# Reordering the opening loads of a one-core kernel: two x tiles side by side, w_in blocks whole behind them, both tiles transposed first, the gate row third on ScalarE's queue

## The chip, the cores and the metric

The kernel runs on one core of a Trainium2 chip. The metric is device time in microseconds (us); several executions of each kernel are compared with executions of the kernel before on the same chip, in the same rounds. Executions are called fast or slow; a slow one is over 1.5% above the fastest of its kernel, and only fast ones are compared.

A few names: PE is TensorE (matmuls), PEld its weight load, ACT ScalarE, DVE VectorE, POOL GpSimd, SP the queue that issues most loads. A name with q (SPq) is an engine's instruction queue. L192 is a source line.

## The reference, cut to what matters

The result is a gated mix of a linear-attention branch and a gMLP branch over x (2048 x 512, bf16). This case is about the first product of the gMLP branch and the gate:

```python
z = _gelu(jnp.einsum('bsd,df->bsf', x, w_in))     # w_in: 512 x 1376, halves z1 | z2
z2 = _layernorm(z[..., Fh:], axis=-1)             # Fh = 688
g = _sigmoid((x * gate_w).sum(-1, keepdims=True))
return g * a + (1 - g) * b                        # a: attention, b: gMLP
```

The contraction runs over 512 = 4 blocks of 128 rows of w_in ("block 0" to "block 3"). x is cut into 16 tiles of 128 rows; each must be transposed before it can be the stationary operand. The gate's weights are a 689th column of w_in's z2 half.

## The kernel before: the parts that matter

Tiles 0 and 1 of x are loaded plainly and transposed on TensorE; tiles 2 and later come through transposing loads.

```python
nc.gpsimd.dma_start(out=gaterow[0:NDT, :], in_=gate_w...)             # gate row, GpSimd
nc.sync.dma_start(out=xs[:, 0, :], in_=x2[0:P, :])                    # x tile 0
nc.scalar.dma_start(out=w_z2[:, 0, 0:HF], in_=...)                    # block 0, first half
nc.sync.dma_start(out=xs[:, 1, :], in_=x2[P:2 * P, :])                # x tile 1
load_z2w(nc.scalar, 1)                                                # block 1
load_z2w(nc.sync, 2)                                                  # block 2
nc.scalar.dma_start(out=w_z2[:, 0, HF:FH], in_=...)                   # block 0, second half
load_z2w(nc.sync, 3)                                                  # block 3
...
x_dma_T(2, 2)                                                         # x tiles 2 and 3, transposing, SP
# ... w_z1, x tiles 4 to 15, brow, wqkT, eight small w_phi loads, wv, wspT, all on SP
```

The order of TensorE's work on the two tiles is written out by hand. `warm_up` runs matmuls on constants ("fillers") whose results are thrown away; `one(tt, dt, j)` is tile tt, block dt, half j; `z_part` is a part of a second half; `gate_T` transposes the gate row and VectorE copies it into column 689.

```python
warm_up(6)                       # six 128x512 fillers
warm_up(2, P)                    # two 128x128 fillers
x_T(0, 0, 1, ...); x_T(0, 1, NDT, ...)          # tile 0: four transposes
warm_up(3, P)
one(0, 0, 0)
x_T(1, 0, 2, ...); x_T(1, 2, NDT, ...)          # tile 1: four transposes
one(0, 1, 0); warm_up(1, P); one(1, 0, 0); one(1, 1, 0)
for tt in range(2): z_part(tt, 1, 0, HF, True)  # block 1, second half
gate_T()
for tt in range(2): z_part(tt, 0, 0, HF, False) # block 0, second half: the late load
# ... block 2, the gate column of blocks 0 and 1, block 3, outputs; then tile 2, tile 3, ...
```

The softmax here doesn't subtract the row's maximum and nothing guards it: scores larger than these inputs give would overflow.

## Time and profile before

| | before |
|---|---|
| time, median of 3 | 207.25 us (206.95 to 207.43) |
| span of the profiled execution | 205.4 us |
| PE busy | 201.2 us, 98% |
| PE's only wait inside the kernel | 0.47 us, for a load of w_in |

From the profile page: the span, the busy time of the first engines, and the chain of work that ended last, by engine.

```profile
span 205.4 us, 4012 instructions
PE 201.2 (98%) x1564; PEld 120.3 (59%) x1564; DVE 129.8 (63%) x282; ACT 75.4 (37%) x123; POOL 46.4 (23%) x77
...
PE 96%; DMA 2%; ACTq 0%; DVE 0%; issue 0%
```

PE's waits (what waited, for what, total us, times, longest): the first is the start of the program.

```profile
PE zp L223 <- PEq L627: 0.8, 1, 0.8
PE zp L231 <- DMA w_z<-in_B_w_in_dram: 0.5, 1, 0.5
```

So only the opening can be shortened. This is its timeline on PE (start in us, duration, engine and line, operation, count, and in brackets an idle time and what ended it). Matmuls overlap, so the distance between two starts tells the rate, not the duration. L223 are fillers, L285 transposes, L192 and L231 real matmuls, L295 the gate row.

```profile
3.57 0.63 PE L285 MATMUL pq<-ident,xs 128*128 128x128 bf16 x4
4.00 0.45 PE L223 MATMUL zp<-const-bfloat16-1.0 128*128 128x128 bf16 x3
4.28 0.31 PE L192 MATMUL zp<-w_z,xT 128*128 128x344 bf16 x1
4.43 0.27 PE L285 MATMUL tp<-ident,xs 128*128 128x128 bf16 x2
...
5.09 0.46 PE L192 MATMUL zp<-w_z,xT 128*128 128x344 bf16 x2
5.39 0.46 PE L231 MATMUL zp<-w_z,xT 128*128 128x344 bf16 x2
5.68 0.17 PE L295 MATMUL pq<-ident,gaterow 128*128 128x4 bf16 x1
6.32 0.45 PE L231 MATMUL zp<-w_z,xT 128*128 128x344 bf16 x2 [0.47 <-DMA w_z<-in_B_w_in_dram]
...
7.30 0.89 PE L192 MATMUL zp<-w_z,xT 128*128 128x344 bf16 x5
```

The second half of block 0 is issued at 1.74 us and lands at 6.28 us; PE is idle from 5.85 us. Transposes start 0.107 us apart at 3.57 us (four in 0.43 us); by 4.28 us, one 344-wide matmul takes 0.15 us to the next start. The clock rose at about 4.2 us. From 6.32 us on, a 344-wide matmul follows every 0.144 us. The last listed line holds block 3's four matmuls and the first of tile 2, so **tile 2 starts at 7.30 + 4 x 0.144 = 7.88 us**.

### The profile page before, as it was taken

How to read it: one execution, taken by the hardware profiler on the slowest of the kernel's cores; microseconds unless marked ns; L12 is line 12 of the kernel's file. 1: busy time of each engine (PE TensorE's matmuls, PEld its weight loads, DVE VectorE, ACT ScalarE, POOL GpSimd, SP SyncE). 2: the span in 40 equal slices, each digit the busy share in tenths (PEclk: the TensorE clock that was granted, in tenths of full speed). 3: DMA queues.
4: the chain of work that ended last, by engine and by line, in shares of the span. 5: the costliest groups of instructions: out<-in, count | busy, mean ns of one | idle time of the engine just before them, and what ended most of it. 6: DMA issues, size and time to landing. Idle time of an engine off the chain costs nothing.

```text
span 205.4 us, 4012 instructions
## 1 busy us (share of the span) xinstructions
PE 201.2 (98%) x1564; PEld 120.3 (59%) x1564; DVE 129.8 (63%) x282; ACT 75.4 (37%) x123; POOL 46.4 (23%) x77
## 2 busy tenths in 40 slices
PE   8999999999999999999999999999999999999994
PEld 4566666655665555656565666555555555665642
DVE  4377575747977687979797788555566645633330
ACT  3466577796222233332424042222251136002222
POOL 5020202020522425334242442222204220200000
PEclk9999999999999999999999999999999999999999
DMA  6998599999999017940433229763566568552942
GB/s 175 265 183 186 92 212 209 206 259 206 265 245 217 3 38 158 307 91 13 83 29 63 51 38 117 143 117 71 100 161 51 119 114 181 67 97 55 145 89 78
DMA packets 90100, 27.22 MB, mean 133 GB/s; under 512 B 84225, under 2 KB 90081, under 8 KB 90081
## 3 DMA queue, kind: packets, MB, share of 16 engines
q1 hardware_dynamic: 87312, 24.55, 64.1%
q10 hardware_dynamic: 2736, 2.42, 4.3%
q8 instruction: 12, 0.20, 0.4%
q14 instruction: 8, 0.06, 0.1%
q0 software_dynamic: 32, 0.00, 0.0%
HBM read 4.15 MB, written 2.10 MB: 30 GB/s over the span
## 4 chain that ended last, share of the span: by engine, by line
PE 96%; DMA 2%; ACTq 0%; DVE 0%; issue 0%
PE mm L459 36%; PE zp L192 18%; PE mm L360 14%; PE mm L520 8%; PE mm L514 7%; PE mm L400 7%; DMA w_z<-in_B_w_in_dram 2%; PE kvacc L416 2%; PE at L472 2%; PE mm L524 1%; PE zp L312 0%; PE at L483 0%; PE zp L231 0%; ACTq L118 0%; ACTq L121 0%; PE pq L312 0%
## 5 line engine op out<-in xcount | busy, mean ns | idle before, releaser
L459 PE MATMUL mm<-z2all,wspT 128*128 128x344 bf16 x512 | 79.9, 309 | 0.0
L459 PEld LDWEIGHTS <-wspT 128*128 128x128 bf16 x512 | 49.0, 98 | 25.3
L192 PE MATMUL zp<-w_z,xT 128*128 128x344 bf16 x252 | 37.9, 309 | 0.1
L364 ACT ACTIVATE eq<-mm 128x512 bf16<-128x512 f32 x32 | 17.4, 594 | 51.4 <-PE mm L360 25.7
L368 DVE TENSOR_REDUCE zs<-eq 128x64 f32<-128x1024 bf16 x16 | 19.5, 1220 | 20.1 <-ACT eq L364 20.1
L192 PEld LDWEIGHTS <-xT 128*128 128x128 bf16 x252 | 24.3, 98 | 12.0 <-DVE xT L291 0.3
L364 ACT ACTIVATE ek<-mm 128x512 bf16<-128x512 f32 x32 | 17.3, 601 | 27.1 <-PE mm L360 27.1
L377 POOL TENSOR_TENSOR eq<-eq,ratio 128x512 bf16<-128x512 bf16 x16 | 16.9, 1056 | 44.6 <-DVE ratio L376 36.7
L464 DVE SCALAR_TENSOR_TENSOR ucat<-mm,bT,z1all 128x344 bf16<-128x344 f32 x32 | 17.4, 544 | 14.9 <-PE mm L459 14.9
L535 ACT ACTIVATE ob<-mm,g_inv 128x512 bf16<-128x512 f32 (+1 forms) x16 | 10.9, 680 | 32.4 <-PE mm L524 26.6
L368 DVE TENSOR_REDUCE zs<-ek 128x64 f32<-128x1024 bf16 x16 | 19.3, 1209 | 2.8 <-ACT ek L364 2.8
L520 PE MATMUL mm<-wspT,uT 128*128 128x512 bf16 (+2 forms) x85 | 20.1, 367 | 0.0
L360 PEld LDWEIGHTS <-xT 128*128 128x128 bf16 x128 | 12.2, 98 | 12.0
L377 POOL TENSOR_TENSOR ek<-ek,ratio 128x512 bf16<-128x512 bf16 x16 | 16.9, 1056 | 2.2 <-DVE ratio L376 1.7
L514 PE MATMUL mm<-wspT,oT 128*128 128x512 bf16 (+2 forms) x68 | 16.6, 366 | 0.0
L360 PE MATMUL mm<-wq_p,xT 128*128 128x512 bf16 x64 | 16.4, 379 | 0.0
L400 PE MATMUL mm<-wv_sb,xT 128*128 128x512 bf16 x64 | 16.4, 379 | 0.0
L360 PE MATMUL mm<-wk_p,xT 128*128 128x512 bf16 x64 | 16.3, 379 | 0.0
L210 DVE BATCH_NORM_STATS2 bn<-z2all 128x6 f32<-128x344 bf16 x32 | 14.9, 503 | 0.0
L207 ACT ACTIVATE z2all<-zp 128x688 bf16<-128x688 f32 x16 | 11.8, 743 | 7.8 <-PE zp L192 7.7
L265 ACT ACTIVATE z1all<-zp 128x688 bf16<-128x688 f32 x16 | 11.9, 743 | 5.1 <-PE zp L192 4.7
L520 PEld LDWEIGHTS <-uT 128*128 128x128 bf16 x85 | 8.1, 98 | 9.4 <-issue 0.2
(78 smaller groups left out, 145.3 us busy)
## 6 DMA issues: line engine op xcount, KB each, us to landing
out_dram<-ob ACTq DMA_DIRECT2D x15, 128.0 KB, 2.2
wspT<-in_B_w_out_dram SPq DMA_DIRECT2D x2, 640.0 KB, 5.0
w_z<-in_B_w_in_dram SPq DMA_DIRECT2D x2, 344.0 KB, 4.8
wv_sb<-in_A_wqkv_dram SPq DMA_DIRECT2D x2, 256.0 KB, 3.6
wspT<-in_A_wo_dram SPq DMA_DIRECT2D x2, 256.0 KB, 4.0
w_z<-in_B_w_in_dram SPq DMA_DIRECT2D x2, 172.0 KB, 4.2
xs<-in_A_x_dram SPq DMA_DIRECT2D x2, 128.0 KB, 2.7
uT<-ucat SPq DMA_TRANSPOSE x16, 2.8
```

Source lines behind the costliest of these rows:

```text
L192: nc.tensor.matmul(zp[:, j, 0:n], lhsT=xT[:, dt, tt * P:(tt + 1) * P], rhs=wt[:, dt, j * HF:j * HF + n], start=(dt == first), stop=(dt == ...
L210: nc.vector.bn_stats(out=bn6[:, tt, j, :], in_=z2v[:, j, :])
L265: nc.scalar.activation(out=z1all[:, tt, :].rearrange("p (j n) -> p j n", j=2), in_=zp[:, :, 0:HF], func=AF.Gelu_apprx_tanh,)
L360: nc.tensor.matmul(ps[:, :], lhsT=xT[:, dt, tt * P:(tt + 1) * P], rhs=w[:, dt, :], start=(dt == 0), stop=(dt == NDT - 1))
L364: nc.scalar.activation(out=e[:, :, a, :], in_=ps[:, :].rearrange("p (h f) -> p h f", f=DH), func=AF.Exp, scale=1.0 - 2.0 * a)
L368: nc.vector.tensor_reduce(out=z[:].rearrange("p h a -> p (h a)"), in_=e[:].rearrange("p h a f -> p (h a) f"), axis=AX.X, op=ALU.add,)
L377: nc.gpsimd.tensor_tensor(out=e[:, :, 1, :], in0=e[:, :, 1, :], in1=ratio[:, :, None].to_broadcast([P, H, DH]), op=ALU.mult)
L400: nc.tensor.matmul(v_ps[:, :], lhsT=xT[:, dt, tt * P:(tt + 1) * P], rhs=wv_sb[:, dt, :], start=(dt == 0), stop=(dt == NDT - 1))
L459: nc.tensor.matmul(gp[:, 0:HF], lhsT=wspT[:, st, tt * P:(tt + 1) * P], rhs=z2all[:, st, j * HF:(j + 1) * HF], start=(st == 0), stop=(st == ...
L464: nc.vector.scalar_tensor_tensor(out=ucat[tt % NU][:, c0 + j * HF:c0 + (j + 1) * HF], in0=gp[:, 0:HF], scalar=bT[:, tt:tt + 1], in1=z1all[ ...
L514: nc.tensor.matmul(acc, lhsT=oTs[tt][:, g, :], rhs=wo_t[:, g, c0:c1], start=start and g == 0, stop=stop and g == NG - 1)
L520: nc.tensor.matmul(acc, lhsT=uTs[tt][:, i + ft, :], rhs=w_main[i][:, ft, c0:c1], start=start and ft == 0, stop=False)
```

## The change

Its intent: bring both x tiles in first, side by side on two queues, so that both can be transposed in one go; load block 0 whole, so that no late half stands in the way; move the gate row from GpSimd to ScalarE's queue, third; and drop fillers and the split matmuls that the late half needed. Long parts are cut.

```diff
-    nc.gpsimd.dma_start(out=gaterow[0:NDT, :], in_=gate_w...)
     nc.sync.dma_start(out=xs[:, 0, :], in_=x2[0:P, :])
-    nc.scalar.dma_start(out=w_z2[:, 0, 0:HF], in_=w_in_v[:, 0, FH:FH + HF])
-    nc.sync.dma_start(out=xs[:, 1, :], in_=x2[P:2 * P, :])
+    nc.scalar.dma_start(out=xs[:, 1, :], in_=x2[P:2 * P, :])
+    load_z2w(nc.sync, 0)
     load_z2w(nc.scalar, 1)
     load_z2w(nc.sync, 2)
-    nc.scalar.dma_start(out=w_z2[:, 0, HF:FH], in_=w_in_v[:, 0, FH + HF:F])
+    nc.scalar.dma_start(out=gaterow[0:NDT, :], in_=gate_w...)
     load_z2w(nc.sync, 3)
 ...
         warm_up(6)
-        warm_up(2, P)
+        warm_up(1, P)
         x_T(0, ...)
-        warm_up(3, P)
-        one(0, 0, 0)
         x_T(1, ...)
+        warm_up(2, P)
+        one(0, 0, 0)
+        z_part(0, 0, HF, True)
         one(0, 1, 0)
-        warm_up(1, P)
         one(1, 0, 0)
+        gate_T()
+        z_part(1, 0, HF, True)
         one(1, 1, 0)
         for tt in range(2):
-            z_part(tt, 1, 0, HF, True)
-        gate_T()
+            one(tt, 1, 1)
 ...     # then block 2 and block 3, in nearly the same order as before
```

## The prediction

> **What bounds it.** On the profile page PE is busy 98% of the 205.4 us span, and the chain of waits is 96% PE. The waits view of PE knows one wait inside the kernel: 0.47 us for a w_in DMA. Only the opening, until tile 2 begins, can shrink; the rest should shift with it.
>
> **The opening before** (timeline; DMA view, issue plus time to landing). Warm-ups run from 0.85 to 3.57 us. Landings, us: x tile 0 3.4; first half of w_in block 0 3.5; x tile 1 4.1; block 1 4.2; gate row 5.6; block 2 5.8; second half of block 0 6.3; block 3 6.5; x tiles 2 and 3 (transposing) 7.5. Real matmuls start at 4.28, broken up by tile 1's transposes and fillers; PE stops at 5.85 for the late half block, resumes at 6.32, and from there a matmul follows every 0.144 us. Tile 2 begins near 7.87. The two tiles need 16 such matmuls, 2.3 us.
>
> **What changes.** The same bytes before the transposing loads (966 KB at 260 to 300 GB/s, windows view, 2 to 5 us), in another order and on other queues. The Trainium skill, "DMA: Bandwidth & Descriptors", "Issuing engines are not separate DMA queues", says that loads issued on several engines share the same 16 DMA engines; so I expect no bandwidth from the move. Removed: the late half block, the gate row's GpSimd work (0.76 us, POOL idle anyway), two fillers, two tiny matmuls (0.03 us each). Added: the first real matmul waits for the whole block 0.
>
> Estimated landings, from cumulative bytes on the measured ones: x tiles 3.5 to 3.7 both; blocks 0 and 1 4.6 to 4.8; gate row 4.8 to 5.3; block 2 5.8; block 3 6.4; x tiles 2 and 3 7.4 to 7.5.
>
> PE, estimated: both tiles transposed by 4.4; first real matmul 4.65; gate matmul 5.2; its copy (0.24 us until it starts, 0.18 long) reaches PE near 5.7, after matmuls to 5.55, so a new gap of 0.1 to 0.2 us; block 1's second halves until 6.0, block 2 6.6, block 3 7.2. Tile 2 then finds its x not landed and waits to about 7.45. The kernel gains 7.87 - 7.45, about 0.4 us, where the first two tiles gain 0.65. w_z1's halves land at 8.8 and 9.6, needed at 9.75 and 10.3: no wait.
>
> **Predicted:** 207.25 - 0.37 = 206.9 us, range 206.5 to 207.4. Faster by over 2%: 0.005; within: 0.99; slower: 0.005.
>
> **What would show each step.** (1) No wait for w_in near 5.9 us. (2) First real matmul at 4.5 to 4.8 us, a short idle before it. (3) A gap of 0.1 to 0.2 us behind the gate's copy. (4) The two tiles' last matmul near 7.2; then a wait for the x transpose until 7.4 to 7.5. (5) Later stages as long as before, shifted by 0.4 us.
>
> **What would make it wrong.** The gate row lands at 5.6 as before: gain 0.25. Block 0 lands after 5.1: gain under 0.1. The clock: "TensorE: Matmul & The Clock Gate", Part 1, says that the default state is throttled and activity releases it; the trace shows 512-wide fillers 0.43 us apart before about 4 us, 344-wide matmuls 0.144 us apart after 4.3. If idling near 4.5 us delays the release, up to 1 us is lost. If tile 2's x lands before 7.4, the gain rises to 0.65. Run-to-run scatter is 0.5 us, as large as the effect.

## The result, and the profile after

Ratios here and below are the mean time of one kernel's fast runs over the mean of the other's fast runs of the same rounds, so not quite the ratio of the medians quoted.

| | before | after |
|---|---|---|
| median of 6 | 207.34 us (206.93 to 207.74) | 206.70 us (206.21 to 206.96) |
| ratio, 95% interval | | 0.9967 (0.9948 to 0.9986) |
| span, profiled | 205.4 us | 205.0 us |

The same change was measured twice more (a_again, a_third below): 0.9979 and 0.9985. The three ratios average 0.9977; of 207 us that is about 0.5 us.

The page, and PE's waits:

```profile
span 205.0 us, 3998 instructions
...
PE 98%; DVE 0%; issue 0%
```

```profile
PE zp L222 <- PEq L623: 0.8, 1, 0.8
```

The wait for w_in is gone, and so is the DMA share of the chain. The opening on PE (L222 fillers, L281 transposes, L191 and L230 real matmuls, L291 the gate row):

```profile
3.52 0.61 PE L281 MATMUL pq<-ident,xs 128*128 128x128 bf16 x4
3.92 0.42 PE L281 MATMUL tp<-ident,xs 128*128 128x128 bf16 x2
...
4.34 0.42 PE L222 MATMUL zp<-const-bfloat16-1.0 128*128 128x128 bf16 x2
4.56 0.49 PE L191 MATMUL zp<-w_z,xT 128*128 128x344 bf16 x1
4.84 0.49 PE L230 MATMUL zp<-w_z,xT 128*128 128x344 bf16 x1
5.13 0.64 PE L191 MATMUL zp<-w_z,xT 128*128 128x344 bf16 x2
5.61 0.17 PE L291 MATMUL pq<-ident,gaterow 128*128 128x4 bf16 x1
5.63 0.31 PE L230 MATMUL zp<-w_z,xT 128*128 128x344 bf16 x1
5.78 1.03 PE L191 MATMUL zp<-w_z,xT 128*128 128x344 bf16 x5
...
7.00 1.18 PE L191 MATMUL zp<-w_z,xT 128*128 128x344 bf16 x7
```

The first four real matmuls start 0.29 us apart (4.56, 4.84, 5.13, and the next at 5.42), twice the 0.144 us of those after 5.63 us. In this execution the clock rose only at about 5.5 us, 1.3 us later than in the profile before. (Not every 0.29 us is a low clock: the pause from 5.78 to 6.07 us is twice 0.145 us, one matmul and a wait for the gate's copy, with the clock already up.) Tile 2 starts at 7.00 + 4 x 0.144 = 7.58 us, 0.30 us earlier than before. From there on the kernel is the same, moved: one of the last full groups of spatial-product matmuls, for instance, starts at 183.13 us instead of 183.43 us.

The late rise is a finding that the prediction had only among its risks. Is it caused by the new order of work on TensorE, or is it chance? If it is caused by the order, the change could be improved by putting fillers back. That is the first question of the experiments.

### The profile page after: what moved, and what is told of

The parts are those of the page before. It is cut to its first block, busy times and chain, and to the rows that moved or that the text cites. A ratio compares the mean times of both kernels' runs of the same rounds, so it can differ in the third digit from the quotient of the medians.

```text
span 205.0 us, 3998 instructions
## 1 busy us (share of the span) xinstructions
PE 201.4 (98%) x1559; PEld 120.3 (59%) x1559; DVE 129.7 (63%) x282; ACT 75.5 (37%) x123; POOL 45.6 (22%) x76
## 4 chain that ended last, share of the span: by engine, by line
PE 98%; DVE 0%; issue 0%
PE mm L455 36%; PE zp L191 18%; PE mm L356 14%; PE mm L516 8%; PE mm L510 7%; PE mm L396 7%; PE kvacc L412 2%; PE at L468 2%; PE zp L222 1%; PE mm L520 1%; PE zp L308 0%; PE pq L281 0%; PE at L479 0%; PE zp L230 0%; PE pq L308 0%; DVE ob L527 0%
## 5 line engine op out<-in xcount | busy, mean ns | idle before, releaser
L191 PE MATMUL zp<-w_z,xT 128*128 128x344 bf16 (+1 forms) x254 | 38.5, 311 | 0.0
L191 PEld LDWEIGHTS <-xT 128*128 128x128 bf16 x254 | 24.6, 98 | 12.2 <-issue 0.2
```

The lines of the kernel that those rows point to most:

```text
L191: nc.tensor.matmul(zp[:, j, 0:n], lhsT=xT[:, dt, tt * P:(tt + 1) * P], rhs=wt[:, dt, j * HF:j * HF + n], start=(dt == 0), stop=(dt == NDT ...
```

## The experiments

**Theory A**: the new order delays the rise, because eight transposes stand in a row and fewer fillers run. **Rival B**, later called the chance-clock theory: the moment of the rise varies from execution to execution whatever the order, and each microsecond of delay costs the changed kernel about half a microsecond, because matmuls at half rate advance half as fast.

### First set: both kernels again, fillers back, loads alone (one chip)

**a_again**: the changed kernel, no edit.

> The changed kernel again, unmodified. In its first profile the TensorE clock rose only near 5.55 us (344-wide matmuls 0.29 us apart until then), in the kernel before near 4.2 us. Theory A (the new PE order, eight transposes in a row and fewer fillers, delays the rise): again 5.4 to 5.7 us, span 205.0. Rival B (the moment of the rise is chance, from execution to execution): another moment, anywhere between 4.1 and 6 us, and spans of the timed runs that scatter over 0.6 us or more, 204.4 to 205.2, as half-rate matmuls come and go.

Measured: 206.58 us median, ratio to before 0.9979 (0.9960 to 0.9998). The rise came at about 6.6 us, later even than the 6 us that rival B allowed: read one by one (narrow windows of the timeline), matmuls start at 6.15, 6.44, 6.67 and 6.82 us, so the distance is still 0.287 us from the first to the second, 0.234 from the second to the third and 0.148 after that (the line at 6.44 us is from such a window, the others from a wide one):

```profile
5.26 0.78 PE L191 MATMUL zp<-w_z,xT 128*128 128x344 bf16 x2
...
5.91 0.45 PE L230 MATMUL zp<-w_z,xT 128*128 128x344 bf16 x1
6.15 1.12 PE L191 MATMUL zp<-w_z,xT 128*128 128x344 bf16 x5
...
6.44 0.40 PE L191 MATMUL zp<-w_z,xT 128*128 128x345 bf16 x1
...
7.46 0.75 PE L191 MATMUL zp<-w_z,xT 128*128 128x344 bf16 x4
```

Tile 2 starts at 7.46 + 0.58 = 8.04 us, later than in the kernel before's first profile, and the span of this one execution is 205.4 us, the same as before's. The spans of the six executions run from 204.5 to 205.6 us.

**b_again**: the kernel before, no edit.

> The kernel before again, unmodified. Theory A: the clock rises again near 4.2 us and the span is 205.4. Rival B: the rise comes at another moment, up to 6 us, and where it comes later the wait for the late half block hides part of it, since PE idles from 5.85 to 6.32 us anyway; spans scatter less than those of the changed kernel.

Measured: 207.25 us, ratio 1.0006 (0.9990 to 1.0021), as it should be for the same kernel. But its clock rose at about 5.5 us, not at 4.2 us, with the order of work unchanged:

```profile
4.61 0.42 PE L285 MATMUL tp<-ident,xs 128*128 128x128 bf16 x2
4.82 0.42 PE L285 MATMUL pq<-ident,xs 128*128 128x128 bf16 x2
5.03 0.49 PE L192 MATMUL zp<-w_z,xT 128*128 128x344 bf16 x1
5.32 0.31 PE L223 MATMUL zp<-const-bfloat16-1.0 128*128 128x128 bf16 x1
...
6.26 0.45 PE L231 MATMUL zp<-w_z,xT 128*128 128x344 bf16 x2
...
7.24 1.04 PE L192 MATMUL zp<-w_z,xT 128*128 128x344 bf16 x6
```

The rise was 1.3 us later than in the first profile of the same kernel, yet tile 2 starts at 7.24 + 0.58 = 7.82 us, as early as before (7.88). The late half of block 0 lands at about 6.2 us anyway; TensorE, slow, now gets there only shortly before (the gate matmul stands at 6.07 us) instead of waiting from 5.85 us. The wait of the kernel before is slack that hides a late rise. The changed kernel has no such slack. The spans agree: b_again's six run from 205.2 to 205.8 us, a_again's from 204.5 to 205.6. Theory A falls as the cause of a late rise: the kernel before has one too. That the order shifts how often a rise is late can't be excluded with nine profiles.

**a_fill3**: fillers between the transposes instead of behind them.

```diff
+        warm_up(3, P)
         x_T(1, ...)
-        warm_up(2, P)
         one(0, 0, 0)
```

> The changed kernel with three 128-wide fillers between the two tiles' transposes in place of two behind them. Theory A: the rise comes near 4.2 us as in the kernel before, the four half-rate matmuls (0.29 us each) become 0.144 us, and the kernel is 0.4 to 0.6 us faster than the changed one: span 204.5. Rival B: rise at a chance moment, mean of the timed runs within 0.15 us of the changed kernel's.

Measured: its profiled execution was slow (236.3 us, granted clock 0.854) and is left out of the timing. The other five average 206.97 us; the ratio is 0.9993 (0.9973 to 1.0012). Theory A's gain of 0.4 to 0.6 us on the changed kernel is not there. Nor is its rise near 4.2 us: the opening of that profile is still at half rate at 5.89 us (0.287 us from start to start), though a slow execution is weak support. The version is 0.3 us worse than a_again (206.69), which rival B did not expect either, with one filler more on the path and intervals that overlap.

**b_loads**: the new loads under the old order on TensorE (the first hunk of the change alone, with the old program below).

> The new loads alone (x tile 1 first on ScalarE, block 0 whole on SP, gate row third on ScalarE) under the kernel before's PE order. Both theories: the 0.47 us wait near 5.9 us goes. If the loads carry the whole gain, the span is 204.9 or less; if the new PE order is needed, it stays near 205.4. Theory A adds that with this order the clock rises near 4.2 us, so this version should beat the changed kernel by about 0.3 us; rival B does not.

Measured: 206.82 us, ratio 0.9989 (0.9974 to 1.0003); no wait for w_in; rise at about 6.0 us, tile 2 at 7.95 us. Theory A wanted a rise near 4.2 us and a version 0.3 us faster than the changed kernel; its mean is 0.2 us above a_again's. The point estimate is 0.2 us of gain by the loads alone and as much again by the new order, which removes three fillers (0.107 us each at the low rate); the intervals are too wide to split it more finely.

### Second set: loads held back, fewer fillers, the gate row's queue (another chip)

**a_hot and b_hot**: all loads but the eight of w_phi held back until the clock is surely up. Both kernels got the same edit:

```diff
+    nc.vector.memset(z2all[:], 0.0)
+    nc.vector.memset(z1all[:], 0.0)
+    # one element of each held load's destination is written from those, so each load waits for them
-        warm_up(6)
+        warm_up(57)
```

> The changed kernel with all its loads held back by about 13 us (two long VectorE memsets before them) and 57 instead of 6 fillers 512 wide, so that the TensorE clock is up in every execution long before the first x tile lands. Chance-clock theory: every matmul of the first two tiles is 0.144 us behind the last one where its data are there; tile 2's first matmul comes 6.0 to 6.6 us after the first load is issued (it was 6.8 and 7.2 us in the two profiles with a late rise), bounded by x tiles 2 and 3 or by the gate's copy; the timed runs scatter by under 0.4 us, where the changed kernel's scattered by 1.2. Rival (the scatter comes from the loads' landing): scatter as before, about 1 us.

> The kernel before held back in the same way. Chance-clock theory: the wait for the late half of block 0 is there in full, tile 2 starts about 7.0 us after the first load is issued, and this kernel is 0.5 to 0.9 us slower than a_hot, more than the 0.3 to 0.7 us between the unheld kernels. If the loads' order gives no gain of its own, the two are equal within 0.2 us.

Measured: a_hot 219.90 us median (219.78 to 221.52), b_hot 221.12 us (220.01 to 222.30); the means are 220.31 and 221.14 us, so 0.83 us apart. The difference is of the size that the chance-clock theory named, but the intervals of the two ratios overlap (1.0591 to 1.0651 and 1.0618 to 1.0682), so it isn't shown. a_hot's tile 2 starts 6.2 us after its first load, as expected. b_hot's starts 8.7 us after it (13.94 to 22.64 us), not 7.0, and no wait for the late half of block 0 is listed. Nor did the scatter shrink: it is 1.7 and 2.3 us, not 0.4. The edit has a flaw: TensorE idles while it waits for x and w_in, and the clock can fall again. In b_hot's profile, after an idle 0.91 us and then 1.15 us, matmuls are at half rate again (17.02 us is before the second wait; the pair at 19.06 us is followed at 19.63, 0.29 us for each):

```profile
17.02 0.32 PE L203 MATMUL zp<-w_z,xT 128*128 128x344 bf16 x1
...
18.71 0.44 PE L203 MATMUL zp<-w_z,xT 128*128 128x344 bf16 x1 [1.15 <-DMA w_z<-in_B_w_in_dram]
...
19.06 0.78 PE L203 MATMUL zp<-w_z,xT 128*128 128x344 bf16 x2
19.63 0.78 PE L242 MATMUL zp<-w_z,xT 128*128 128x344 bf16 x2
```

So this pair shows what the changed kernel does with the clock up (a_hot's profile), but it is no comparison of the two kernels at a high clock, and doesn't isolate the clock from the landing of the loads.

**a_nofill**: the two fillers before the first real matmul removed.

```diff
-        warm_up(2, P)
         one(0, 0, 0)
```

> The changed kernel without the two fillers between the transposes and the first real matmul. Chance-clock theory: while the clock is low the transposes end as late as block 0 lands, so the fillers cost 0.21 us on the chain and removing them gains up to 0.2 us on the changed kernel (206.4 us); with the clock up it gains nothing. Rival (fillers bring the rise forward): 0.1 us slower or more.

Measured: 207.10 us, ratio 0.9992 (0.9956 to 1.0028); inconclusive, with one execution at 209.14 us. Its profile is worth more than its times. Among the profiles whose loads are not held back, it is the only one with the new loads in which the clock rose early, at or before 4.5 us:

```profile
4.54 0.31 PE L191 MATMUL zp<-w_z,xT 128*128 128x344 bf16 x1
4.69 0.31 PE L230 MATMUL zp<-w_z,xT 128*128 128x344 bf16 x1
4.83 0.45 PE L191 MATMUL zp<-w_z,xT 128*128 128x344 bf16 x2
...
6.51 2.21 PE L191 MATMUL zp<-w_z,xT 128*128 128x344 bf16 x14
```

Tile 2 starts at 6.51 + 0.58 = 7.09 us, 0.8 us earlier than in the kernel before. And yet the span is 205.4 us. PE's waits in this profile, without that of the start, say why:

```profile
...
PE pq L307 <- DMA wphi<-in_A_w_phi_dram: 0.7, 1, 0.7
```

At 25.9 us TensorE comes to the products with w_phi, whose eight small loads are issued on SP behind the transposing loads. The last one was issued at 25.1 us in this execution and lands 1.6 us later. In the profile before, the last was issued at 24.0 us and the products started at 26.7 us. So there is a second deadline, and an early start can be given back there. But two things met here. In the seven other profiles of the table below with w_phi on SP, its last load landed at 24.6 to 25.9 us, 0.7 to 2.3 us before the products started; here it landed at 26.7 us. With a landing at 24.9 us, as in the profile after, the early start would have met no wait. Why the loads were issued late in this execution was not tested.

**a_gatepool**: the gate row back on GpSimd.

```diff
-    nc.scalar.dma_start(out=gaterow[0:NDT, :], in_=gate_w...)
+    nc.gpsimd.dma_start(out=gaterow[0:NDT, :], in_=gate_w...)     # where it was before
```

> The changed kernel with the gate row loaded by GpSimd again, as before. It landed at 5.4 to 5.6 us that way and the gate matmul comes fifth, at 5.2 (clock up early) to 5.9 us (late rise): equal to the changed kernel within 0.15 us when the rise is late, up to 0.3 us slower when it is early; so the median 0 to 0.2 us slower. If it is 0.3 us slower or more, the gate row's queue carries a large part of the gain.

Measured: 206.91 us, ratio 0.9975 (0.9956 to 0.9993), as good as the changed kernel's own ratios. The gate row's queue carries no gain that these runs can see.

### Third set: a version without the second deadline, a control, and both kernels without fillers (a third chip)

**a_best**: no fillers before the first real matmul, and w_phi on GpSimd.

```diff
-    for u in range(8): nc.sync.dma_start(out=wphi[us, :, us], in_=heads[u])
 ...
-        warm_up(2, P)
 ...
             z2_norm(ts)
+            if c == 0:
+                # wphi = 0 * rstd on GpSimd, then the eight loads
+                for u in range(8): nc.gpsimd.dma_start(out=wphi[us, :, us], in_=heads[u])
```

> The changed kernel without the two fillers before the first real matmul, and with w_phi's eight small loads on GpSimd behind the first normalisation (14 to 21 us) instead of on SP at 20 to 25 us, because a_nofill, whose clock rose at 4.4 us and whose tile 2 started at 7.1 us, then waited 0.7 us for w_phi at 25.9 us. Theory: no wait for w_phi in any execution, so an early start is no longer given back; median 0.1 to 0.4 us under the changed kernel's, 206.2 to 206.5 us. Rival (w_phi never mattered but in that one slow execution): equal to the changed kernel within 0.15 us.

**a_third**: the changed kernel, no edit, as the control.

> The changed kernel, unmodified, as the control beside a_best, a_cold and b_cold. 206.6 us median, runs from 206.2 to 207.3; in the profile span minus the start of tile 2 is 197.4 to 197.5 us as in the profiles so far, and the start of tile 2 follows half the moment of the clock's rise.

Measured: a_best 206.62 us, ratio 0.9979 (0.9965 to 0.9993); a_third 206.92 us, ratio 0.9985 (0.9969 to 1.0001). a_best is 0.16 us faster in the mean (206.66 against 206.82); the intervals overlap almost wholly, so that it beats the changed kernel isn't shown. a_best's profile has no wait for w_phi, but its clock rose late, at about 6.5 us (tile 2 at 7.79 us), so it didn't come under the deadline's pressure. In a_third, the rise was at about 6.1 us, tile 2 at 7.24 + 0.58 = 7.82 us, span 205.3 us.

**a_cold and b_cold**: every filler removed from the changed kernel and from the kernel before.

> The changed kernel without any filler: TensorE does nothing until x tile 0 lands at 3.5 us. Chance-clock theory: the rise needs some 3.4 us of activity, so it comes after 6.9 us in every execution; all 16 matmuls of the first two tiles are 0.29 us apart, tile 2 starts at 8.9 us or later and its own matmuls may be slow too: 1.2 to 3 us slower than the changed kernel. Rival (the clock does not depend on the fillers): equal to it within 0.3 us.

> The kernel before without any filler. Chance-clock theory: at half rate TensorE itself is later than every load, the late half of block 0 makes no wait, and the change gains nothing: b_cold and a_cold are equal within 0.3 us. Rival (the loads' order gains by itself, whatever the clock): b_cold 0.3 to 0.7 us slower than a_cold.

Measured: without one execution of 428 us (see the last section), a_cold's five average 208.11 us, ratio 1.0049 (1.0031 to 1.0067); b_cold's six 207.75 us, ratio 1.0031 (1.0014 to 1.0049). Removing the fillers costs the changed kernel 1.3 us against a_third and the kernel before 0.6 us against its own runs (207.10). The change then gains nothing. The rival, that the loads' order gains whatever the clock, is out: it wanted b_cold 0.3 to 0.7 us slower than a_cold, and its mean is 0.36 us lower (the intervals overlap, so that it is faster isn't shown). That is a little more than the "equal within 0.3" of the chance-clock theory. A likely reason, argued from one line, is that the half block lets the kernel before start real work at 3.96 us, while TensorE is the slower party:

```profile
3.96 0.47 PE L192 MATMUL zp<-w_z,xT 128*128 128x344 bf16 x1
```

b_cold does still show a wait of 0.32 us for the late half, which the theory had not expected. Its clock rose at about 8.9 us, 5.6 us after its first transpose, and tile 2 starts at 9.28 us; the theory's "some 3.4 us of activity" is only the shortest distance seen (0.85 to 4.2 us in the first profile). a_cold has no profile of a fast execution.

### All profiles side by side

The rise is put inside the first matmul whose distance to the next lies between 0.287 and 0.145 us, with the starts read one by one.

| profile | rise of the clock, about | tile 2 starts | span | span minus tile 2 |
|---|---|---|---|---|
| before | 4.2 | 7.88 | 205.4 | 197.5 |
| b_again | 5.5 | 7.82 | 205.3 | 197.5 |
| b_loads | 6.0 | 7.95 | 205.4 | 197.5 |
| after | 5.5 | 7.58 | 205.0 | 197.4 |
| a_third | 6.1 | 7.82 | 205.3 | 197.5 |
| a_again | 6.6 | 8.04 | 205.4 | 197.4 |
| a_gatepool | 6.5 | 7.97 | 205.5 | 197.5 |
| a_best | 6.5 | 7.79 | 205.3 | 197.5 |
| a_nofill | 4.5 or before | 7.09 | 205.4 | 198.3 |

The last column is a constant but for a_nofill, which lost 0.7 us to w_phi. So what the change is worth is decided before tile 2. In the kernel before, tile 2's start hardly depends on the rise (7.88 and 7.82 us for rises 1.3 us apart). In the changed kernels it does: 7.09 us with an early rise, 7.58 us with a rise at 5.5, 8.04 us with one at 6.6, so 0.46 us for 1.1 us. (a_best and a_gatepool rise together; a_best, with two fillers fewer, starts tile 2 0.18 us earlier.) The gain is therefore a mixture, about 0.8 us with an early rise and about nothing with a rise at 6 us. How often each comes these profiles can't say: in a_again, b_loads, a_gatepool, a_best and a_third the profiled execution is the slowest or second slowest of its six. For rises after 5.5 us there is no profile of the kernel before. That the changed kernel's fastest executions (spans of 204.5 and 204.6 us) are the early ones is an inference: 7.09 + 197.45 = 204.5 fits, but those executions have no profile.

## Why the prediction was right or wrong, point by point

- **The bound and the place.** Right. Only the opening changed; everything after tile 2's start is as long as before, moved by 0.30 us in the first pair of profiles.
- **Step 1, no wait for w_in near 5.9 us.** Right.
- **Step 2, first real matmul at 4.5 to 4.8 us.** Right in time (4.56 us), but not for the stated reason. Block 0, issued at 1.27 us, landed after 3.0 us, at 4.2 us, not 4.6 to 4.8. TensorE was not idle; it was still on the last transpose and two fillers at half rate.
- **Step 3, a gap of 0.1 to 0.2 us behind the gate's copy.** Right: the copy ends at 5.84 + 0.18 = 6.02 us; the second matmul after the gate starts at 5.78 us and would let the next follow at 5.93, which starts at 6.07 us.
- **Step 4, a wait at tile 2 for x tiles 2 and 3 until 7.4 to 7.5 us.** This is the step that failed. There is no such wait in any profile with the new loads. Those tiles landed 4.1 us after their issue at 2.67 us, at 6.7 us; in a_nofill tile 2 started at 7.09 us without waiting. What bounded TensorE was its clock: the first four matmuls took 1.05 us (4.56 to 5.61) instead of 4 x 0.144 = 0.58, a term of about 0.5 us that the prediction held as a risk ("If idling near 4.5 us delays the release, up to 1 us is lost") and not in the sum. Without it tile 2 would have started near 7.1 us, by this estimate, as in a_nofill. The risk's reason wasn't met either: no idle time is listed near 4.5 us. The other risk, "if tile 2's x lands before 7.4", came true with it.
- **The loads.** "No bandwidth from the move" was wrong by some 10%. The prediction leaned on the Trainium skill, "DMA: Bandwidth & Descriptors", section "Issuing engines are not separate DMA queues": loads issued on several engines share the same 16 DMA engines. That may well hold, but the change also loads block 0 in one piece. From 2 to 5 us (each engine's busy time, then clock, DMA share and GB/s) two profiles with the old loads moved 278 and 292 GB/s, here the first and the second of before:

```profile
2.00:5.00 3.00, 3.00 (x20) 1.78 (x18) 1.14 (x5) 1.64 (x3) 1.34 (x10) 1.00 0.95 278
```

```profile
2.00:5.00 3.00, 3.00 (x18) 1.94 (x17) 0.88 (x4) 1.49 (x2) 1.34 (x10) 1.00 0.96 292
```

  and the one after 324:

```profile
2.00:5.00 3.00, 3.00 (x17) 1.79 (x16) 1.07 (x5) 1.86 (x3) 0.60 (x5) 1.00 0.96 324
```

  Eight more with the new loads gave 297 to 320 (a_fill3 297, a_gatepool 305, a_again 307, a_nofill 311, a_third 313, b_loads 316, a_cold 319, a_best 320; a_fill3 and a_cold are slow executions), and b_cold, with the old ones, 290. The landings agree: block 3, the last of these loads, landed at 6.4 to 6.9 us in the three old profiles and at 5.6 to 6.2 us in the nine new ones. a_gatepool, with the gate row on GpSimd, is above all old ones, so the gate row isn't the whole cause. Rows of 688 bytes became rows of 1376; whether that is the cause was not tested.
- **The size.** 207.25 - 0.37 = 206.9 us was predicted, 206.7 us measured, inside the range; three measurements average a gain of about 0.5 us. The two errors, x tiles too late and the clock too early, nearly cancelled (tile 2 predicted near 7.45, measured 7.58 us). The number was right by luck; the limit named for it was not.

## What to carry to other kernels

Before removing a wait at the start of a kernel, ask what else it hides: here the wait for a late load absorbed a late rise of TensorE's clock, so removing it gained 0.8 us in the one profile with an early rise and 0.3 us or less in the others. Read the clock from the distance between matmul starts, in more than one profile of the same kernel, before giving a cause to a difference of half a microsecond. And after moving a start forward, look for the next deadline downstream (w_phi here, 0.7 to 2.3 us behind in seven profiles), because the gain can be handed back there.

## What the Trainium skill lacked or had wrong

- "TensorE: Matmul & The Clock Gate", Part 1, says that the default state is throttled and activity releases it, around 4 us into sustained activity, +-500 ns, by a free-running window. The runs agree that it varies, over more: in nine profiles the rise came between 4.2 and 6.6 us with fillers from 0.85 us on, that is 3.4 to 5.8 us into activity. What the page lacks is that a wait in the opening can hide a late rise: in the kernel before tile 2 starts at 7.88 and 7.82 us with rises at 4.2 and 5.5 us.
- The same part holds the loss small and speaks of a clock seen stuck at a low ratio for over 50 us. One execution of a_cold was slow from its start to its end: span 426.4 us, 344-wide matmuls listed at 523 ns instead of 309. This isn't the half rate of the openings: read one by one, starts alternate 0.26 and 0.37 us apart (0.32 us in the mean, as in the line with 40 of them below, not 0.29), and a few follow after 0.145 us (4.93 and 5.08 us), as with the clock up. It was one of twelve executions without fillers (six of a_cold, six of b_cold); that the missing fillers cause it isn't shown. The granted clock stood at 1.00 in the record:

```profile
span 426.4 us, 3980 instructions
...
8.64 12.66 PE L191 MATMUL zp<-w_z,xT 128*128 128x344 bf16 x40
...
L452 PE MATMUL mm<-z2all,wspT 128*128 128x344 bf16 x512 | 166.8, 523 | 0.0
```

- None of the pages I read says that the granted clock in the profile shows neither that state nor the low clock of the openings: it reads 1.00 in the first microseconds of every profile, also where fillers 512 wide are 0.43 us apart.
- The same page, Part 4, says that the raised clock doesn't engage for transposes on TensorE. Here they follow it: 0.107 us apart at 3.57 us in the kernel before, and after the rise the pair listed at 4.43 us starts 0.05 us apart (4.43 and 4.48). Whether transposes alone would raise it no run shows.

```profile
4.48 0.22 PE L285 MATMUL tp<-ident,xs 128*128 128x128 bf16 x1
```

- "DMA: Bandwidth & Descriptors": nothing in "Issuing engines are not separate DMA queues" is contradicted. With the new loads, block 0 in one piece among them, the rate was 297 to 324 GB/s, with the old ones 278 to 292; which part of the change did that was not tested.
